# The scrap output of a sum of squares: from the row tile's lo half to the scrap tile of the weights

## Chip, core and metric

One core of a Trainium2 chip runs the whole kernel in one launch. The metric is the device time of the launch in microseconds, the median of several runs. The engines are PE (TensorE, matmuls), DVE (VectorE), ACT (ScalarE), POOL (GpSimd) and SP (SyncE, which here issues the DMAs).

## What is computed

Attention, then a mixture of experts (MoE) that is summed over all experts, then a SoLU block; from the reference:

```python
# 4 batches, 8 heads, 576 rows, head size 64; row block i sees blocks j <= i of 64
scores = scale * np.matmul(q, k.transpose(0, 1, 3, 2))
scores = np.where(mask, scores, -1000000000.0)
attn = np.exp(scores - max); attn = attn / (sum + 1e-09)
x = np.matmul(attn, v)                      # as 2304 rows x 512
p = domain_probs / (domain_probs.sum(-1, keepdims=True) + 1e-09)
for e in range(4):
    out += p[:, e:e + 1] * (np.maximum(x @ w1[e], 0.0) @ w2[e])   # 512 -> 1024 -> 512
# SoLU: h = x @ w_in; ln = layernorm(h * softmax(h)) * g_ln; return ln @ w_out
```

## The kernel before

Rows come in 18 tiles of 128 (`TILES`). Numbers that need more than 16 bits are kept as two F16 tiles, hi and lo, and a product is three matmuls (hi hi, hi lo, lo hi). Before such a split the data are multiplied by a power of two that follows from their sum of squares. That sum is what `squares` makes: ScalarE's Square, whose elementwise output is scrap and whose `accum_out` is the sum. `scale_bits` turns the sum into the power of two on VectorE (L136, L140, L143). `squares` is called from three places around the change: for the weights (`w_steps`, L212: four squares of 128x1024 for each matrix, and then L217, L219 and L221 add the four sums on VectorE and over the partitions with a matmul into the tile `tp`), for the values of attention (L859), and for the rows that attention delivers (`finish`, L1070). The first two write their scrap to `junk`, one tile of 128x1024 BF16 in a pool of one buffer. Rows of x2 later go through `split_rows` (L470), which has its scrap in a row tile too.

Attention goes by steps of two heads (four heads for the first two tiles). A step has scores (`sps`, L920 to L925), their maximum (L935 or L938) and its scaled negative `nm` (L939), exponentials into `sps` or `p32` (L979), the halves `hl` (hi L992 on ScalarE, lo L993 on VectorE), a transposing DMA `hl` to `pT`, and the products with the values (`pv`, L1021). When a tile's four steps are done, `finish` makes its MoE input in three parts: `rows` divides (`xf`, L1063), `scale` takes the squares, and `split` writes the halves into `xh` (hi L1074 on ScalarE, lo L1075 on VectorE) and sends `xh` by a transposing DMA to `xT`. `xh` comes from the pool `fp` of one buffer, so all 18 tiles share one place.

The MoE phases follow expert by expert: `hps` (L375) is the first product, `hch` (L385, L386) its halves, `ops` (L397) the second product, `acc` (L417 or L422) the sum. The weights are loaded into `stage` in four parts, and their halves are made by L231 (GpSimd) or L235 (ScalarE) with L238 (VectorE). GpSimd also splits keys, queries and values (L798, L800, L881). While attention lasts, a planner (`at1.step`, costs `tpe` and `tdv`) decides how attention's steps, the MoE units and the weights' steps follow each other in the program; it is a function of costs written into the kernel and does not look at the scrap tile. Behind it the framework's scheduler, which plays the program through a timeline of its own, chooses the order of instructions on each engine, from the dependences between tiles and the priorities. The squares' scrap is a tile like any other to it: an instruction that writes a tile waits for all who still read or write what was in that place. DMAs of SyncE stay in one order per queue that the scheduler fixes too.

Of the kernel before, what the change touches and what calls it, by code (L numbers as in the profile page):

```python
# [10 lines left out]
BF16 = mybir.dt.bfloat16  # L11
# [52 lines left out]
def tile_kernel(  # L64
# [63 lines left out]
    def squares(x, out, junk=None):  # L128

        if junk is None:  # L130
            junk = jp.tile([128, 1024], BF16, tag="junk", name="junk")[:, :x.shape[1]]
        return act.activation(out=junk, in_=x, func=AF.Square, accum_out=out)

    def scale_bits(T, bits, s, inv):

        vec.tensor_scalar(  # L136
            out=inv.bitcast(I32), in0=T.bitcast(I32), scalar1=24, scalar2=23,
            op0=ALU.logical_shift_right, op1=ALU.logical_shift_left,
        )
        vec.tensor_scalar(  # L140
            out=inv, in0=inv, scalar1=2.0 ** (64 - bits), scalar2=2.0 ** -75, op0=ALU.mult, op1=ALU.max
        )
        vec.reciprocal(out=s, in_=inv)  # L143
# [197 lines left out]
    def xtile(d, t, name):  # L341
        g, c = group(t)
        if g not in d:
            n = GROUPS[g[0]][g[1]][1]
            d[g] = xps[g[0]].tile([128, 2 * KD, 128 * n], F16, tag=f"xT{g[1]}", name=name)
        return d[g][:, :, c:c + 128]
# [397 lines left out]
    class Attention:  # L744
# [300 lines left out]
        def finish(self, t):  # L1045

            b, i = TILES[t]
            inv = sp.tile([128, 1], F32, tag="xi", name="xi")
            xf = self.fp.tile([128, NH, HD], F32, tag="xf", name="xf")
            x = xf.rearrange("p h d -> p (h d)")  # L1050
            xh = self.fp.tile([128, 2, 512], F16, tag="xh", name="xh")
            s = sp.tile([128, 1], F32, tag="xs", name="xs")

            def rows():
                ps, sums = self.xps.pop(t), self.sums.pop(t)
                rs = sp.tile([128, NH, 1], F32, tag="rs", name="rs")
                vec.tensor_scalar(
                    out=rs[:, :, 0], in0=sums, scalar1=1e-9 * 2.0 ** PBITS, scalar2=self.vSc[("z", b) if i == 0 else b],
                    op0=ALU.add, op1=ALU.mult,
                )  # L1060
                ri = sp.tile([128, NH, 1], F32, tag="ri", name="ri")
                vec.reciprocal(out=ri, in_=rs)
                vec.tensor_tensor(  # L1063
                    out=xf, in0=ps.rearrange("p (h d) -> p h d", h=NH), in1=ri.to_broadcast([128, NH, HD]),
                    op=ALU.mult,
                )

            def scale():
                T = sp.tile([128, 1], F32, tag="xt", name="xt")
                squares(x, T, xh[:, 1].bitcast(BF16))  # L1070
                scale_bits(T, 4, s, inv)

            def split():
                act.activation(out=xh[:, 0], in_=x, func=AF.Copy, scale=s)  # L1074
                vec.scalar_tensor_tensor(  # L1075
                    out=xh[:, 1], in0=x, scalar=s, in1=xh[:, 0], op0=ALU.mult, op1=ALU.subtract
                )
                sync.dma_start_transpose(out=xtile(xT, t, "xT"), in_=xh.rearrange("p a f -> p (a f)"))
                vec.tensor_scalar_mul(pt[:, t, :], pn[:, t, :], inv)

            return [rows, scale, split]


# [536 lines left out]
```

## Time and profile before

| | |
|---|---|
| runs | 1089.95, 1090.99, 1091.23 us, median 1090.99 |
| profiled execution | 1090.29 us, its span 1088.5 us |
| mean granted TensorE clock | 0.997 |
| busy: PE, DVE, ACT, POOL | 1041.5, 776.3, 511.1, 208.1 us |
| read from HBM, written | 79.47 MB, 12.06 MB |

The span is the time from the first to the last instruction in the trace; the profiled execution's own time is 1.8 us longer. Busy time is a sum over the whole span; where an engine waits has to be looked up by stretches. A share of 96% for TensorE leaves some 47 us in which it does nothing.

### The profile page before, as it was taken

How to read it: one execution, taken by the hardware profiler on the slowest of the kernel's cores; microseconds unless marked ns; L12 is line 12 of the kernel's file. 1: busy time of each engine (PE TensorE's matmuls, PEld its weight loads, DVE VectorE, ACT ScalarE, POOL GpSimd, SP SyncE). 2: the span in 40 equal slices, each digit the busy share in tenths (PEclk: the TensorE clock that was granted, in tenths of full speed). 3: DMA queues.
4: the chain of work that ended last, by engine and by line, in shares of the span. 5: the costliest groups of instructions: out<-in, count | busy, mean ns of one | idle time of the engine just before them, and what ended most of it. 6: DMA issues, size and time to landing. Idle time of an engine off the chain costs nothing.

```text
span 1088.5 us, 20680 instructions
## 1 busy us (share of the span) xinstructions
PE 1041.5 (96%) x8088; PEld 657.0 (60%) x8088; DVE 776.3 (71%) x1758; ACT 511.1 (47%) x1108; POOL 208.1 (19%) x280
## 2 busy tenths in 40 slices
PE   4679899999999999999899999999999999999998
PEld 4556666656655655655476777776766674444444
DVE  6879677748767765545786557665879558999883
ACT  5757578546755454532353334231446353323322
POOL 4967733534237311000000000000000000000000
PEclk9989999999999999999999999999999999999999
DMA  9978997566677865235331211330346312435233
GB/s 295 277 175 167 241 201 189 143 173 172 158 178 174 186 112 129 56 90 157 122 97 51 77 47 55 117 136 30 98 145 167 77 24 36 88 88 106 60 87 87
DMA packets 225745, 137.96 MB, mean 127 GB/s; under 512 B 184560, under 2 KB 193008, under 8 KB 225648
## 3 DMA queue, kind: packets, MB, share of 16 engines
q1 hardware_dynamic: 225648, 136.65, 50.3%
q8 instruction: 63, 1.03, 0.4%
q14 instruction: 34, 0.28, 0.1%
HBM read 79.47 MB, written 12.06 MB: 84 GB/s over the span
## 4 chain that ended last, share of the span: by engine, by line
PE 84%; DMA 6%; DVE 4%; POOL 3%; ACT 1%; issue 1%; SPq 0%; DVEq 0%; ACTq 0%; POOLq 0%
PE ops L397 31%; PE hps L629 14%; PE hps L375 14%; PE o L1536 9%; PE h L1470 9%; PE pv L1021 3%; DMA pT<-hl 3%; PE sps L920 2%; PE sps L923 2%; DMA xT<-xh 1%; POOL ks L800 1%; DMA raw<-in_w_dram 1%; DMA x2T<-xh 1%; DMA near<-in_kT_dram 1%; DMA vraw<-in_vC_dram 1%
## 5 line engine op out<-in xcount | busy, mean ns | idle before, releaser
L397 PE MATMUL ops<-wt,hch 128*128 128x512 f16 x1728 | 393.1, 379 | 2.4 <-DVE wt L238 1.4
L397 PEld LDWEIGHTS <-hch 128*128 128x128 f16 x1728 | 166.1, 98 | 187.4 <-issue 6.7
L375 PE MATMUL hps<-xT,wt 128*128 128x384 f16 (+1 forms) x1536 | 216.1, 290 | 6.3 <-DVE hch L386 3.9
L375 PEld LDWEIGHTS <-wt 128*128 128x128 f16 x1536 | 126.5, 100 | 64.4 <-issue 6.1
L979 ACT ACTIVATE p<-sps,nm 128x320 f32<-128x320 f32 (+3 forms) x120 | 70.1, 587 | 85.1 <-DVE nm L939 75.4
L993 DVE TENSOR_TENSOR hl<-p,hl 128x320 f16<-128x320 f32 (+3 forms) x120 | 75.6, 650 | 37.3 <-ACT hl L992 37.2
L629 PEld LDWEIGHTS <-S 128*128 128x128 f16 x1152 | 96.0, 98 | 3.0 <-issue 0.9
L1536 PE MATMUL o<-wt,lt 128*128 128x512 f16 (+1 forms) x456 | 95.6, 368 | 0.0
L1470 PE MATMUL h<-wt,x2T 128*128 128x512 f16 x432 | 95.5, 379 | 0.0
L238 DVE SCALAR_TENSOR_TENSOR wt<-stage,ws,wt 128x1024 f16<-128x1024 f32 (+1 forms) x64 | 82.9, 1304 | 7.4 <-ACT wt L235 4.3
L422 DVE SCALAR_TENSOR_TENSOR acc<-ops,coef,acc 128x512 f32<-128x512 f32 x54 | 40.4, 748 | 66.4 <-PE ops L397 66.3
L920 PE MATMUL sps<-ks,qhi 128*128 128x288 f32 (+3 forms) x160 | 69.1, 433 | 10.7 <-DVE hl L993 7.5
L629 PE MATMUL hps<-T,S 128*128 128x192 f16 x864 | 76.3, 246 | 0.0
L629 PEld LDWEIGHTS <-wt 128*128 128x128 f16 x864 | 72.8, 98 | 5.8
L642 ACT ACTIVATE stu<-hps 128x384 f32<-128x384 f32 x72 | 34.6, 482 | 86.5 <-PE hps L629 86.3
L1536 PEld LDWEIGHTS <-lt 128*128 128x128 f16 x456 | 44.6, 98 | 48.9
L1470 PEld LDWEIGHTS <-x2T 128*128 128x128 f16 x432 | 42.3, 98 | 51.0
L386 DVE SCALAR_TENSOR_TENSOR hch<-hps,hch 128x384 f16<-128x384 f32 (+1 forms) x98 | 52.8, 540 | 21.9 <-ACT hch L385 21.8
L647 ACT ACTIVATE hch<-stc 128x384 f16<-128x384 f32 x72 | 37.4, 521 | 63.5 <-DVE stc L655 63.2
L385 ACT ACTIVATE hch<-hps 128x384 f16<-128x384 f32 (+1 forms) x98 | 46.9, 481 | 39.5 <-PE hps L375 39.4
L1021 PE MATMUL pv<-v,pT 128*128 128x64 f16 x1392 | 56.6, 196 | 8.9 <-DMA pT<-hl 8.8
L1021 PEld LDWEIGHTS <-pT 128*128 128x128 f16 x1392 | 51.6, 100 | 20.5 <-DMA pT<-hl 10.8
(163 smaller groups left out, 1534.6 us busy)
## 6 DMA issues: line engine op xcount, KB each, us to landing
stage<-in_w_dram SPq DMA_DIRECT2D x50, 512.0 KB, 5.9
raw<-in_qT_dram SPq DMA_DIRECT2D x34, 256.0 KB, 3.1
vraw<-in_vC_dram SPq DMA_DIRECT2D x30, 256.0 KB, 3.2
raw<-in_kT_dram SPq DMA_DIRECT2D x24, 288.0 KB, 3.5
raw<-in_w_dram SPq DMA_DIRECT2D x24, 256.0 KB, 4.1
raw<-in_w_in_dram SPq DMA_DIRECT2D x8, 512.0 KB, 4.7
raw<-in_w_out_dram SPq DMA_DIRECT2D x8, 512.0 KB, 4.2
stage<-wf SPq DMA_DIRECT2D x8, 512.0 KB, 6.6
```

The lines of the kernel that those rows point to most:

```text
L238: stage["last"] = vec.scalar_tensor_tensor(out=lo, in0=r, scalar=stage[key, "s"], in1=hi, op0=ALU.mult, op1=ALU.subtract)
L375: pe.matmul(ps[:, j * n:j * n + n], w[:, a, kk, f * 128:(f + 1) * 128], x[:, b * KD + kk, c0:c0 + n], start=(m == 0), stop=(m == 3 * KD - 1),)
L385: marks["A"] = nc.scalar.activation(out=h[:, 0, :n], in_=ps[:, :n], func=AF.Relu)
L386: marks["D"] = nc.vector.scalar_tensor_tensor(out=h[:, 1, :n], in0=ps[:, :n], scalar=0.0, in1=h[:, 0, :n], op0=ALU.max, op1=ALU.subtract)
L397: pe.matmul(ps, hch[f][:, a, o0:o0 + 128], w[:, b, f, :], start=(m == 0), stop=(m == 3 * KF - 1))
L629: i = pe.matmul(ps[x][:, jj * HT:jj * HT + HT], lhs(a, kk, jj), rhs(b, kk), start=start, stop=(m == 5), skip_group_check=not first or jj > 0,)
L920: pe.matmul(o, q, rhs, start=True, stop=False)
L979: act.activation(out=src if direct else dst, in_=src, func=AF.Exp, bias=nm[:, j + x:j + x + 1], scale=SCALE, accum_out=sums[:, h:h + 1],)
L993: anc["D"] = vec.tensor_tensor(out=lo, in0=pf, in1=hi, op=ALU.subtract)
L1021: pe.matmul(o, tt[:, a * nch + c, :], v[:, bb, hs], start=(m == 0), stop=(m == total - 1))
L1470: pe.matmul(ps[:, half], x[:, a * KD + kk, c:c + 128], w[:, b, kk, half * 512:half * 512 + 512], start=(m == 0), stop=(m == 3 * KD - 1),)
L1536: pe.matmul(ps, tt[:, x * KF + f], w[:, y, f, c], start=(m == 0), stop=(m == 3 * KF - 1))
```

## The change

One line in `finish`: the squares of a tile's 128x512 rows no longer name a place for their scrap, so `squares` takes the first 512 columns of `junk`. Number, engine, size and type of the 18 squares are as before.

```diff
             def scale():
                 T = sp.tile([128, 1], F32, tag="xt", name="xt")
-                squares(x, T, xh[:, 1].bitcast(BF16))
+                squares(x, T)
                 scale_bits(T, 4, s, inv)
```

So the square no longer writes `xh`: it need not wait until the DMA of the previous tile has read `xh`, and the lo half (L1075) need not wait for it as a writer of the same bytes. It writes `junk` instead, behind the square that wrote `junk` before it, on the same engine. With these dependences the scheduler's order differs on every engine, from about 35 to 230 us by the clock of before: on PE in rows 132 to 3136 of 15778, on DVE up to row 335 of 1760, on ACT up to 229 of 850, on POOL from 35 up to 132 of 285, on SP up to 129 of 391. Behind that the engines' rows are the same. Tiles are numbered in order of their making, and each `finish` now makes one more, so that names differ by a few: `sps_1228` of before is `sps_1232`, `hl_1269` is `hl_1273`, `tp_1390` is `tp_1394`, `stage_1116` is `stage_1119`, `pT_1501` is `pT_1505`.

ScalarE, before, at 43 us in the trace: the squares of the first weight matrix of expert 1 (`stage_1116`), two of the four shown, among the steps of the third and fourth tile.

```order
L979 ACTIVATE sps_602,sums_509<-sps_602,nm_603 128x192
L132 ACTIVATE junk_1232,wt4_1117<-stage_1116 128x1024
L132 ACTIVATE junk_1317,wt4_1117<-stage_1116 128x1024
L979 ACTIVATE sps_651,sums_509<-sps_651,nm_652 128x192
L132 ACTIVATE xh_533,xt_540<-xf_532 128x512
L992 ACTIVATE hl_618<-sps_602 128x192
L992 ACTIVATE hl_703<-sps_651 128x192
```

ScalarE in the change, at the place where `finish` of a later tile has its square (`junk_1211` from `xf_1202`): here stand the four squares of that matrix (`stage_1119`), with the exponentials of `sps_1232` between.

```order
L132 ACTIVATE junk_1211,xt_1210<-xf_1202 128x512
L417 ACTIVATE acc_1311<-ops_1286,c0_1284 128x512
L132 ACTIVATE junk_1236,wt4_1120<-stage_1119 128x1024
L132 ACTIVATE junk_1321,wt4_1120<-stage_1119 128x1024
L979 ACTIVATE p32_1274,sums_1084<-sps_1232,nm_1233 128x448
L979 ACTIVATE p32_1278,sums_1084<-sps_1232,nm_1233 128x448
L1074 ACTIVATE xh_1203<-xf_1202,xs_1204 128x512
L132 ACTIVATE junk_1323,wt4_1120<-stage_1119 128x1024
L992 ACTIVATE hl_1273<-p32_1274 128x448
L992 ACTIVATE hl_1273<-p32_1278 128x448
L132 ACTIVATE junk_1325,wt4_1120<-stage_1119 128x1024
L979 ACTIVATE p32_1336,sums_1084<-sps_1319,nm_1320 128x448
```

The four squares moved some fifty rows back on ScalarE, from rows 44, 45, 56 and 58 to rows 93, 94, 98 and 101.

VectorE, before: the sum over the four squares' results (L217, `wt1_1388`), at 57.81 us in the trace.

```order
L386 SCALAR_TENSOR_TENSOR hch_656<-hps_655,hch_656 128x384
L238 SCALAR_TENSOR_TENSOR wt_560<-stage_268,ws_270,wt_560 128x1024
L386 SCALAR_TENSOR_TENSOR hch_656<-hps_724,hch_656 128x384
L217 TENSOR_REDUCE wt1_1388<-wt4_1117 128x1
L935 TENSOR_REDUCE sps_777<-sps_777 128x2
L386 SCALAR_TENSOR_TENSOR hch_780<-hps_779,hch_780 128x256
```

VectorE in the change, the same instruction (`wt1_1392`), behind the maximum of `sps_1390` and the lo halves of `hl_1273`.

```order
L1075 SCALAR_TENSOR_TENSOR xh_1203<-xf_1202,xs_1204,xh_1203 128x512
L938 TENSOR_REDUCE nm_1391<-sps_1390 128x1
L939 TENSOR_SCALAR nm_1391<-nm_1391 128x1
L993 TENSOR_TENSOR hl_1273<-p32_1274,hl_1273 128x448
L993 TENSOR_TENSOR hl_1273<-p32_1278,hl_1273 128x448
L217 TENSOR_REDUCE wt1_1392<-wt4_1120 128x1
L221 COPY wt2_1396<-tp_1394 128x1
```

PE, before: the matmul that reads it, into `tp_1390`, between the scores `sps_1315` and the first product `hps_1450` of expert 1.

```order
L920 MATMUL sps_1315<-ks_440,qhi_1021 128x448
L923 MATMUL sps_1315<-ks_440,qlo_1022 128x448
L925 LDWEIGHTS mr_88
L925 MATMUL sps_1315<-mc_89,mr_88 128x64
L920 MATMUL sps_1315<-ks_443,qhi_1021 128x448
L923 MATMUL sps_1315<-ks_443,qlo_1022 128x448
L925 LDWEIGHTS mr_88
L925 MATMUL sps_1315<-mc_89,mr_88 128x64
L219 MATMUL tp_1390<-wt1_1388,ones_87 128x1
L375 LDWEIGHTS wt_415
L375 MATMUL hps_1450<-xT_477,wt_415 128x128
```

PE in the change: the same matmul, into `tp_1394`, behind the products of `pT_1181` and the scores `sps_1390`.

```order
L1021 LDWEIGHTS pT_1181
L1021 MATMUL pv_1346<-v_459,pT_1181 128x64
L920 MATMUL sps_1390<-ks_396,qhi_1221 128x288
L923 MATMUL sps_1390<-ks_396,qlo_1222 128x288
L925 LDWEIGHTS mr_88
L925 MATMUL sps_1390<-mc_89,mr_88 128x64
L920 MATMUL sps_1390<-ks_396,qhi_1221 128x288
L923 MATMUL sps_1390<-ks_396,qlo_1222 128x288
L219 MATMUL tp_1394<-wt1_1392,ones_87 128x1
L375 LDWEIGHTS wt_415
L375 MATMUL hps_1454<-xT_478,wt_415 128x128
```

It moved behind 48 products with `pT_1094` and `pT_1181` and behind `sps_1390`, and stands ahead of `hps_1454` as before. A little earlier on PE the 24 matmuls of `ops_1282` stand before as 8 behind `sps_1114`, 14 behind `sps_1228` and 2 behind the products of `pT_1001`; in the change as 11 ahead of `sps_1117` (`sps_1114` of before), 11 behind it, and 2 behind `sps_1232`.

SyncE, before: the transposes of attention's halves (`pT`) and the loads of the second weight matrix of expert 1 (`stage_2501`, four parts of 512 KB), at 100 to 123 us in the trace.

```order
L94 DMA_TRANSPOSE pT_1340<-hl_1331 128x14x128
L94 DMA vraw_1636<-in_vC_dram 128x512
L94 DMA_TRANSPOSE pT_1501<-hl_1406 128x18x128
L94 DMA raw_1790<-in_qT_dram 128x512
L94 DMA stage_2501<-in_w2_dram 128x2x512 x2
L94 DMA raw_1658<-in_kT_dram 128x576
L94 DMA stage_2501<-in_w2_dram 128x2x512 x2
L94 DMA raw_1738<-in_kT_dram 128x576
L94 DMA_TRANSPOSE pT_1651<-hl_1584 128x18x128
L94 DMA_TRANSPOSE xT_1214<-xh_1615 128x8x128
```

SyncE in the change (`stage_2508`; `pT_1505` is `pT_1501` of before):

```order
L94 DMA_TRANSPOSE pT_1282<-hl_1273 128x14x128
L94 DMA_TRANSPOSE pT_1344<-hl_1335 128x14x128
L94 DMA raw_1536<-in_kT_dram 128x576
L94 DMA vraw_1641<-in_vC_dram 128x512
L94 DMA stage_2508<-in_w2_dram 128x2x512 x3
L94 DMA_TRANSPOSE pT_1505<-hl_1410 128x18x128
L94 DMA_TRANSPOSE xT_1218<-xh_1619 128x8x128
L94 DMA_TRANSPOSE pT_1656<-hl_1588 128x18x128
L94 DMA raw_1663<-in_kT_dram 128x576
L94 DMA raw_1743<-in_kT_dram 128x576
```

Three of the four parts moved ahead of that transpose, the fourth behind three more transposes; `vraw` and `raw` loads moved among them.

## Rows read from the trace of the kernel before

**Rows 1.** The page: engines' busy time, and what the chain that ended last consists of.
```profile
PE 1041.5 (96%) x8088; PEld 657.0 (60%) x8088; DVE 776.3 (71%) x1758; ACT 511.1 (47%) x1108; POOL 208.1 (19%) x280
...
PE 84%; DMA 6%; DVE 4%; POOL 3%; ACT 1%; issue 1%; SPq 0%; DVEq 0%; ACTq 0%; POOLq 0%
```

**Rows 2.** Stretches: start:end and length, busy us (x instructions) by engine, PEclk, DMA share, GB/s.
```profile
53.00:71.00 18.00, 11.93 (x113) 7.65 (x109) 14.74 (x27) 9.85 (x29) 17.38 (x16) 1.00 0.61 122
71.00:77.00 6.00, 5.23 (x47) 4.59 (x47) 3.78 (x8) 4.01 (x12) 2.73 (x4) 0.50 1.05 276
77.00:103.00 26.00, 26.00 (x347) 19.84 (x345) 22.20 (x49) 21.26 (x51) 14.69 (x19) 0.98 0.84 182
103.00:106.00 3.00, 0.72 (x18) 0.46 (x17) 3.00 (x4) 1.95 (x4) 2.91 (x4) 1.00 0.76 130
106.00:123.00 17.00, 17.00 (x204) 13.07 (x199) 15.92 (x35) 9.96 (x22) 13.88 (x20) 1.00 1.00 251
123.00:135.00 12.00, 8.23 (x150) 6.75 (x148) 4.39 (x12) 5.40 (x20) 9.21 (x17) 1.00 1.15 218
151.00:1088.50 937.50, 929.34 (x6823) 567.09 (x6820) 657.94 (x1487) 415.47 (x846) 101.89 (x146) 1.00 0.44 110
```

**Rows 3.** TensorE's waits, 98 to 152 us: total us, times, longest.
```profile
PE pv L1021 <- DMA pT<-hl: 5.9, 4, 2.3
PE hps L375 <- DMA xT<-xh: 1.9, 1, 1.9
```

**Rows 4.** Chain that ended last, 76 to 150 us: start, us, what.
```profile
82.29 1.73 PE ops L397 x8
...
89.16 0.43 PE ops L397 x2
...
90.57 0.20 PE tp L219 x2
...
92.00 1.42 PE pv L1021 x48
...
114.91 19.15 DMA pT<-hl x3
```

**Rows 5.** The row tile xh: duration min/median/max in ns; idle time before, by releaser.
```profile
L132 ACT ACTIVATE xh<-xf x18: 614/629/646, 31.3 to 490.3; 128x512 bf16<-128x512 f32 x18
...
  DMA xT<-xh: 5.5, 1
```

**Rows 6.** The scrap tile junk, 20 to 110 us, same columns.
```profile
L132 ACT ACTIVATE junk<-vr x5: 620/629/660, 27.2 to 33.0; 128x512 bf16<-128x512 f32 x5
```

**Rows 7.** ScalarE in order of time: start, us, line, tiles, count, idle before.
```profile
43.27 1.06 ACT L132 ACTIVATE junk<-stage 128x1024 bf16<-128x1024 f32 x1
...
87.99 0.63 ACT L979 ACTIVATE p<-sps,nm 128x448 f32<-128x448 f32 x1 [1.16 <-DVE nm L939]
...
89.22 1.04 ACT L992 ACTIVATE hl<-p 128x448 f16<-128x448 f32 x2
90.16 0.68 ACT L417 ACTIVATE acc<-ops,c 128x512 f32<-128x512 f32 x1
...
150.23 0.63 ACT L132 ACTIVATE xh<-xf 128x512 bf16<-128x512 f32 x1 [5.47 <-DMA xT<-xh]
```

**Rows 8.** VectorE in order of time, same columns.
```profile
85.65 1.10 DVE L935 TENSOR_REDUCE sps<-sps 128x2 f32<-128x896 f32 x1 [0.51 <-PE sps L925]
86.66 1.15 DVE L993 TENSOR_TENSOR hl<-p,hl 128x448 f16<-128x448 f32 x2
...
92.23 0.75 DVE L938 TENSOR_REDUCE nm<-sps 128x1 f32<-128x576 f32 x1
```

**Rows 9.** DMA issues, 20 to 140 us: count, median us from issue to landing.
```profile
pT<-hl SPq DMA_TRANSPOSE x23, 4.4
```

**Rows 10.** DMA issues, 110 to 123 us, same columns.
```profile
pT<-hl SPq DMA_TRANSPOSE x1, 9.1
```

**Rows 11.** SyncE's DMA issues in order of time.
```profile
110.31 0.90 SPq L94 DMA_DIRECT2D stage<-in_w_dram  x2
```

## Prediction

> **What bounds the kernel now.** I read the page first. TensorE is busy 96% of the span and holds 84% of the chain that ended last [rows 1], so a change is worth what it adds to or takes from TensorE's waits. The table by stretches says where those are [rows 2]. From 151 us on, 929.34 of 937.50 us are busy: nothing to gain there, and a delay that gets that far reaches the end. The waits that can move lie ahead: 18.00 - 11.93 = 6.07 us in 53 to 71, 3.00 - 0.72 = 2.28 in 103 to 106, 12.00 - 8.23 = 3.77 in 123 to 135 [rows 2], and 1.9 for a row tile's transpose, which ends at 150.2 [rows 3, 7]. Between 77 and 103 TensorE has no wait at all, nor between 106 and 123.
>
> The three stretches have three limits. In 53 to 71 GpSimd is busy 17.38 of 18 us. In 77 to 103 TensorE itself is the limit. In 106 to 135 it is the DMA engines, busy share 1.00 and 1.15 [rows 2], and the chain there is one piece of 19.15 us through three transposing loads [rows 4].
>
> **The edit itself.** The square costs the same in either place: 629 ns into the row tile, 629 ns into junk [rows 5, 6]. What goes is the square's wait until the transposing DMA has read the previous row tile. The trace has that wait once, 5.5 us [rows 5], before the square at 150.23 [rows 7]. At that moment TensorE's own wait of 1.9 us for that same DMA's data ends [rows 3], and that transfer doesn't start sooner because a later tile's square does. The next write of the row tile, L1074, needs the DMA to be done anyway. So the direct gain is 0; its upper bound is the 1.9 us of that wait.
>
> **What moves.** Without that dependence the scheduler lays out 35 to 230 us anew; behind that the engines' rows are the same. The sum is that of the new order, walked with the durations of before.
>
> *36 to 76 us.* ScalarE loses four squares of 128x1024 here (they go to 90 us and later), and VectorE's and GpSimd's work changes places. GpSimd has the same work in 17.38 busy of 18 us, so what it delivers last can't come much earlier. Some tiles come 2 to 3 us sooner, the first quarter of the second weight matrix later. Bounds: a gain of all 6.07 us; a loss of 3.3, if three of GpSimd's operations (17.38 / 16 = 1.09 each) now stand ahead of one that TensorE waits for. I take **-1.0**, near nothing, since the amount of GpSimd's work is the limit and stays.
>
> *77 to 98 us.* Here new waits arise. (a) Eleven matmuls of L397 now stand ahead of sps_1117 (sps_1114 of before). One takes 1.73 / 8 = 0.216 us, so these scores, which ended at 82.29 [rows 4], end 2.4 us later, at 84.7 on the clock of before. Behind them stand one maximum (1.10), two exponentials (0.63 each), the halves (0.5) and a subtraction (0.6) [rows 7, 8]: the hi and lo rows are whole at 88.8 if nothing else lies between, at 90.2 if it takes the 5.5 us that it took before (82.29 to 86.66 + 1.15). The transposing load takes 4.4 us [rows 9], so its data are there from 93.2 to 94.6. TensorE gets to them at about 91.1: its work ahead of them is that of before (48 pv matmuls from 92.00 in 1.42, half of them ahead) less the 1.6 us of tp, hps and sps from 90.4 on that now come later [rows 4]. Wait: 2.1 to 3.5; I take 2.7. (b) Then come five matmuls of sps_1390 and the tp matmul. Before, tp ran at 90.57 without a wait [rows 4], since VectorE had formed its operand long ahead. Now that operand stands behind the maximum of sps_1390 (0.75) and two subtractions (1.15) [rows 8], 1.9 us at least; and it needs the last of the four squares. ScalarE starts their row when the last of 24 matmuls of L397 is done: before these ended at 89.16 + 0.43 [rows 4] and acc started 0.57 later; now they end at 89.8, so acc starts at 90.4. Then acc 0.6, two squares at 1.16, two exponentials 0.55 to 0.63, the copy of the rows 0.7, a square, the halves 1.04, a square with its readout 1.25 [rows 7]: 8.0 us, 98.4. TensorE is there at 93.8 + 0.7 (the other 24 pv) + 0.9 (sps_1390: the 1.6 above without tp and hps) = 95.4. Wait: 2.0 to 4; I take 3.0. Behind tp stand all of hps_1454 and the scores after it, so nothing fills it. Together **+5.7**.
>
> *98 to 106 us.* The 2.28 us for a transposing load at 105.5 shrink, since what feeds it moved less than TensorE did; two short waits of 0.8 and 0.65 stay by the walk. **-0.8** (0 to -2.28). TensorE is then 3.9 us late at 106.
>
> *106 to 135 us.* DMA decides. Before, pT_1501 is issued ahead of the four 512 KB loads that start at 110.31 [rows 11]; now three of the four are ahead of it. From 110.31 to the landing of the last transpose of the chain, 114.91 + 19.15 = 134.06 [rows 4], there are 23.75 us at a full share. The change puts one more transpose into them, and takes out one 256 KB load (1.0 us at the 251 GB/s of this stretch). A transpose takes 4.4 in the median [rows 9]; if half of it lies beside the next one, the landing is 4.4 / 2 - 1.0 = 1.2 later, if none does 3.4. I take 2.3. TensorE comes 3.9 late and waits there for data that are only 2.3 late, so 1.6 of the 5.9 - 2.28 = 3.6 us waited there for pT [rows 2, 3] are given back: **-1.6**. Behind 135 the delay is carried to the end.
>
> Sum: -1.0 + 5.7 - 0.8 - 1.6 = **+2.3 us**. The profiled execution took 1090.29 (span 1088.5) and would take 1092.6; the median of the runs is 0.70 above it, so I expect **1093.3**.
>
> **The rivals.** What a measurement of this kernel can tell from no change is about 0.2%, 2.2 us.
>
> *Given back whole.* If the transpose moved into the full DMA stretch costs nothing there, the landing comes no later, and all of the 3.6 us is given back: +0.3, 1091.3 (1090 to 1092). For it: the total of the transfers hardly changes. Against: the share of 1.00 and 1.15, and the transpose that stood behind the four loads took 9.1 us where 4.4 is the median [rows 9, 10].
>
> *Not given back, or a lower clock.* After the waits of 53 to 71 the granted clock was 0.50 (the 1.2 GHz level) in 71 to 77: 5.23 us of busy time there [rows 2] would be 2.6 at 2.4 GHz. After two waits of 2.7 and 3.0 us close together it could fall again: 2.6 more, and pT_1505 late by 9.1 - 4.4 = 4.7 times three of four loads, 3.5, instead of any give-back. +3.9 + 2.6 is 1097.5; 1095 to 1098. Against: in 103 to 106 TensorE waited 2.28 of 3 us, and the clock stayed at 1.00.
> The Trainium skill (TensorE: Matmul & The Clock Gate, "What's actually happening") has the throttled rate as the default that activity releases, so after idle time the array may run at half rate; the row of 71 to 77 agrees, that of 103 to 106 shows that not every wait does it.
>
> *Faster.* The stretch of 36 to 76 gains more than I allow: with the squares gone from ScalarE and the row tile's lo half sooner, half of the 6.07 us goes (3.0), and the clock doesn't fall in 71 to 77 (2.6). That is -5.6 in place of -1.0, and -2.3 in all: 1088.7. It decides from 3.3 us of gain in that stretch on. For it: the waits of 53 to 71 are the largest that there are, and the order changes on all engines there. Against: GpSimd's 17.38 of 18.
>
> That the edit does nothing at all (the same order) is excluded by the rows of the order.
>
> **Chances.** Forecast, +1 to +4: 0.47 (own range 1092 to 1095; above 0.2% with 0.32, within it 0.15). Given back whole: 0.18 (same 0.15, faster 0.03). Not given back: 0.16, slower. Faster: 0.19 (faster 0.17, same 0.02). So slower 0.48, same 0.32, faster 0.20. The range is 1089.0 to 1097.5: below it lies about half of the faster case (0.10), above it a third of the third one (0.05), so that 0.15 is left out.
>
> **What would show it.** In the trace of the change: no square waits for xT<-xh, and nothing is gained by it at 150; four junk<-stage squares between 90 and 99 where ScalarE is without a pause; a TensorE wait for a pT of about 2.7 us ahead of sps_1390, and one of about 3 us ahead of tp that ends with VectorE's L217; fewer than 3.6 us waited for pT between 123 and 135; from 151 on the same busy share. I am wrong if TensorE is still without a wait between 77 and 98 (then the walk by durations is wrong, and ScalarE's or the load's lag was shorter), if it waits under 3 us between 53 and 71 (the faster case), or if a stretch behind 151 has changed.

## The result, and the profile after

The change makes the kernel slower: 1097.42 us in the median (1095.95 to 1099.37, four runs) beside 1090.47 of the kernel before on the same chip, a ratio of 1.0073 [1.0053, 1.0094], some 8 us (7.0 between the two medians). I had forecast 1093.3 us, +2.3. The time lies in the range (1089.0 to 1097.5) at its upper end, where the rival "not given back, or a lower clock" stands. The profiled execution took 1099.37 us, 2 above the median.

The stretches of the change, with the columns of [rows 2]:

```profile
53.00:71.00 18.00, 13.56 (x149) 9.32 (x147) 14.11 (x25) 6.86 (x22) 17.28 (x16) 1.00 0.71 159
71.00:77.00 6.00, 3.89 (x35) 2.67 (x32) 2.38 (x6) 4.02 (x12) 2.47 (x5) 0.78 0.86 212
77.00:103.00 26.00, 20.72 (x223) 16.17 (x221) 17.35 (x44) 20.35 (x50) 7.43 (x12) 0.76 0.66 144
103.00:106.00 3.00, 2.86 (x34) 2.54 (x32) 2.67 (x3) 3.00 (x5) 1.46 (x3) 0.66 1.24 263
106.00:123.00 17.00, 14.45 (x180) 11.14 (x176) 15.69 (x31) 11.56 (x24) 15.12 (x18) 1.00 0.69 172
123.00:135.00 12.00, 9.61 (x179) 8.89 (x180) 6.60 (x15) 4.81 (x13) 6.40 (x11) 1.00 1.02 217
151.00:1097.60 946.60, 938.39 (x6904) 572.53 (x6901) 666.90 (x1503) 420.36 (x860) 107.50 (x154) 1.00 0.45 111
```

Read the first number after the length (TensorE's busy time) with the granted clock, third from the end. 77 to 103 was 26.00 busy at 0.98; it is now 20.72 at 0.76, so both waits and a low clock are there. 106 to 123 had no wait and has one of 2.55 us. From 151 on 8.2 us are idle, as before (8.2): whatever is lost is lost ahead of that.

TensorE in order of time, the two new waits in brackets:

```profile
94.66 1.36 PE L1021 MATMUL pv<-v,pT 128*128 128x64 f16 x24 [2.49 <-DMA pT<-hl]
...
96.94 0.44 PE L923 MATMUL sps<-ks,qlo 128*128 128x288 f32 x1
100.17 0.59 PE L219 MATMUL tp<-wt,ones 128*128 128x1 f32 x2 [2.79 <-DVE wt L217]
100.62 2.62 PE L375 MATMUL hps<-xT,wt 128*128 128x128 f16 x23
...
123.72 1.05 PE L1021 MATMUL pv<-v,pT 128*128 128x64 f16 x30 [3.27 <-DMA pT<-hl]
```

ScalarE, the row of squares:

```profile
91.29 1.04 ACT L132 ACTIVATE junk<-stage 128x1024 bf16<-128x1024 f32 x1
...
97.31 1.05 ACT L132 ACTIVATE junk<-stage 128x1024 bf16<-128x1024 f32 x1
98.26 0.20 ACT L132 ACTIVATION_READ_ACCUMULATOR junk<-stage 128x1 f32 x1
```

VectorE, what forms the operand of tp:

```profile
97.42 0.76 DVE L938 TENSOR_REDUCE nm<-sps 128x1 f32<-128x576 f32 x1 [1.19 <-PE sps L923]
98.21 0.15 DVE L939 TENSOR_SCALAR nm<-nm 128x1 f32<-128x1 f32 x1
98.29 1.76 DVE L993 TENSOR_TENSOR hl<-p,hl 128x448 f16<-128x448 f32 x2
99.97 0.14 DVE L217 TENSOR_REDUCE wt<-wt 128x1 f32<-128x4 f32 x1
```

SyncE's queue, at the place of the fourth term:

```profile
113.14 1.41 SPq L94 DMA_DIRECT2D stage<-in_w_dram  x3
114.66 6.97 SPq L94 DMA_TRANSPOSE pT<-hl  x1
```

The two waits are the forecast ones, of nearly the forecast size: 2.49 for the transpose (2.7), 2.79 for tp (3.0). The last of the squares ends at 98.46 with its readout, where the walk had 98.4. It is not what ended the wait for tp, though: L217 runs at 99.97, behind the maximum of `sps_1390`, which had waited for TensorE's scores until 97.42, and behind two subtractions of together 1.76 us. And the matmuls between the two waits take longer: a 128x288 product of the scores (L920) takes 0.59 us at 95.83 and 0.38 at 106.49. In each stretch of low clock the granted clock is 0.50, the 1.2 GHz level. Last, pT_1505 behind three loads makes TensorE wait 3.27 us at 123.72.

### The profile page after: what moved, and what is told of

It reads as the page before. It is cut to its first block, busy times and chain, and to the rows that moved or that the text cites. A ratio compares the mean times of both kernels' runs of the same rounds, so it can differ in the third digit from the quotient of the medians.

```text
span 1097.6 us, 20675 instructions
## 1 busy us (share of the span) xinstructions
PE 1044.3 (95%) x8088; PEld 659.3 (60%) x8088; DVE 779.5 (71%) x1758; ACT 512.5 (47%) x1108; POOL 207.6 (19%) x280
## 4 chain that ended last, share of the span: by engine, by line
PE 80%; DMA 6%; DVE 5%; POOL 4%; issue 2%; ACT 1%; SPq 1%; DVEq 0%; POOLq 0%; ACTq 0%
PE ops L397 31%; PE hps L629 14%; PE hps L375 11%; PE o L1536 9%; PE h L1470 8%; DMA pT<-hl 3%; PE pv L1021 3%; PE sps L920 2%; PE sps L923 1%; POOL ks L800 1%; DVE hch L386 1%; POOL ks L798 1%; DMA x2T<-xh 1%; POOL v L881 1%; SPq L94 1%
## 5 line engine op out<-in xcount | busy, mean ns | idle before, releaser
L397 PE MATMUL ops<-wt,hch 128*128 128x512 f16 x1728 | 393.2, 379 | 3.2 <-DVE wt L238 1.7
L397 PEld LDWEIGHTS <-hch 128*128 128x128 f16 x1728 | 166.4, 98 | 188.0 <-issue 7.1
L375 PE MATMUL hps<-xT,wt 128*128 128x384 f16 (+1 forms) x1536 | 219.8, 292 | 2.7 <-DVE hch L386 1.8
L993 DVE TENSOR_TENSOR hl<-p,hl 128x320 f16<-128x320 f32 (+3 forms) x120 | 75.8, 650 | 38.6 <-ACT hl L992 38.2
L920 PE MATMUL sps<-ks,qhi 128*128 128x288 f32 (+3 forms) x160 | 69.8, 437 | 12.3 <-DVE hl L993 7.7
```

The costliest lines, as they stand in the source:

```text
L375: pe.matmul(ps[:, j * n:j * n + n], w[:, a, kk, f * 128:(f + 1) * 128], x[:, b * KD + kk, c0:c0 + n], start=(m == 0), stop=(m == 3 * KD - 1),)
L397: pe.matmul(ps, hch[f][:, a, o0:o0 + 128], w[:, b, f, :], start=(m == 0), stop=(m == 3 * KF - 1))
L920: pe.matmul(o, q, rhs, start=True, stop=False)
L993: anc["D"] = vec.tensor_tensor(out=lo, in0=pf, in1=hi, op=ALU.subtract)
```

## What the order shows, and the theories

Why do four squares of a weight move fifty rows back because a row square changed its scrap? `junk` has one buffer, and the numbers in its names tell the order in which the program makes the tiles: `junk_1211`, tile 3's row square, comes ahead of `junk_1236`, the first square of the weights. Writers of one buffer keep the program's order. Before, the row square wrote elsewhere, and the scheduler let the weights' squares run ahead of it to ScalarE's row 44. In the change they have to wait for tile 3's rows, on row 91.

*Theory A*: this chain of squares, and the order that the scheduler makes from it, costs the time; where the square writes costs nothing. *Rival B*: the freed row tile does it, as the square and the lo half start at other times and the order changes by that. Later runs ask which part of the new order costs: the late squares, the matmuls of L397 ahead of the scores, or the three loads ahead of pT_1505, each by its wait or by the clock.

## The experiments

Times are given as ratios to the kernel before on the same chip with their 95% interval; 0.001 is 1.1 us. In some kernels each engine is bound to a list of its instructions, so that the scheduler lays nothing out anew:

```diff
+    for e, order in pins().items():
+        m = made[e]
...
+        for a, b in zip(order, order[1:]):
+            if b < a or True:
+                after(m[b], m[a])
```

Where a list is edited, the diff shows the move, with the names that stand in it cut short. "Own scrap" is the edit of the first run.

### An own scrap for the rows

```diff
-            junk = jp.tile([128, 1024], BF16, tag="junk", name="junk")[:, :x.shape[1]]
+            junk = jp.tile([128, 1024], mybir.dt.float8e4, tag="junk", name="junk")[:, :x.shape[1]]
...
-                squares(x, T, xh[:, 1].bitcast(BF16))
+                squares(x, T, jp.tile([128, 512], BF16, tag="rows", name="rscrap"))
```

The weights' scrap has 8 bits here, to make room.

> The 18 squares of finish write a scrap tile of their own (the weights' scrap becomes 8-bit to make room for it), so they wait neither for the row tile's DMA nor for the weights' squares. Theory A (one place for all scrap makes the scheduler keep the squares of both kinds in program order, so that the weights' squares of expert 1 stand behind the square of tile 3): they stand early again, no tp wait between 90 and 101, time 1088 to 1093. Rival B (what costs is that the square no longer holds to the row tile, so that everything is laid out anew): 1095 to 1098, as the change.

Measured: 1.0045 [1.0030, 1.0060]. The median, 1096.35 us, lies where rival B had it, and there is no wait for tp, as theory A had it. What came is a third order, which waits 2.28 us for a pT at 150.63 and has the low clock from 151 to 159. So without the chain of squares a new order comes about as well, and it costs some 5 us.

### The chain without the scrap

```diff
-        return act.activation(out=junk, in_=x, func=AF.Square, accum_out=out)
+        prev, marks["sq"] = marks.get("sq"), act.activation(out=junk, in_=x, func=AF.Square, accum_out=out)
+        return after(marks["sq"], prev) or marks["sq"] if prev is not None else marks["sq"]
```

> The kernel before, scrap in the row tile as before, but each square is bound to follow the square before it in the program (an order on ScalarE alone, no wait is added). Theory A: the expert-1 squares stand behind tile 3's, tp waits 2 to 3 us near 97 to 100, time 1094 to 1099. Rival B: the row tile is held as before, so 1089 to 1092.

Measured: 1.0057 [1.0038, 1.0077], with the waits of the change (2.67 for pT, 2.65 for tp), as theory A had it. The scrap stays in the row tile here, so binding the order of the squares alone is enough for the scheduler to make an order with a loss like the change's.

### Which tiles

All but tile 3; tile 3 alone; the first four; the last 14:

```diff
-                squares(x, T, xh[:, 1].bitcast(BF16))
+                squares(x, T, None if t != 3 else xh[:, 1].bitcast(BF16))
...
+                squares(x, T, None if t == 3 else xh[:, 1].bitcast(BF16))
...
+                squares(x, T, None if t < 4 else xh[:, 1].bitcast(BF16))
...
+                squares(x, T, xh[:, 1].bitcast(BF16) if t < 4 else None)
```

> The change in 17 of the 18 tiles; only the square of tile 3 writes to its row tile as before. By the order the four weights' squares then stand behind tile 2's square, some 25 rows of ScalarE earlier than in the change. Theory A: tp's operand is ready in time, no tp wait and no lower clock at 95 to 105, time 1089 to 1094. Rival B: 1095 to 1098, since 17 of 18 row tiles are freed.

> The change in one tile of 18: only the square of tile 3 writes to the weights' scrap. Theory A: the order of the four weights' squares is that of the change, tp waits 2 to 3 us, time 1094 to 1099. Rival B: 1089 to 1092, since 17 of 18 squares are as before.

> The edit in the first four finish tiles only (tiles 0 to 3 write the squares of their rows to the weights' scrap; the 14 later tiles as before). Nothing is bound; the order on every engine comes out as that of the change. If the shared scrap of the first four tiles is the whole cause, the ratio is the change's: 1.006 to 1.009 (1097 to 1100.5). If the 14 later tiles add to it or give some back, it lies outside: below 1.005 or above 1.010.

> The edit in the last 14 of 18 tiles, the first four as before; nothing is bound, and the scheduler's order comes out the same as before on every engine. If only the order costs: 1.000, within 0.2%. If the square's freedom from the row tile's DMA is worth something (the one wait of 5.5 us at 150 is among these 14 tiles): up to 1.9 us faster.

Measured, in this order: 1.0072 [1.0047, 1.0098], 1.0069 [1.0048, 1.0090], 1.0069 [1.0047, 1.0091], 1.0002 [0.9985, 1.0018]. The last 14 tiles keep the order of before on every engine and cost nothing. The first four have the change's order on every engine, name by name but for the numbers, and its time: they carry the whole of it. Theory A missed twice here. Without tile 3 there is no tp wait, as it had it, but a fourth order with a pT wait of 4.70 us at 151.84, and the loss did not go. With tile 3 alone the time is the forecast one, but not its cause: the four squares are as late as in the change (the last ends at 98.8), and still TensorE does not wait for tp. It waits for GpSimd's `qlo` (2.67 us at 95.13) and for transposes (2.60 at 99.27, 3.16 at 129.03).

### The order of before, with the squares freed

Own scrap, and every engine bound to the order of before.

> As e1_own (the rows' squares have a scrap tile of their own, nothing waits for the row tile's DMA), but every engine and the DMA queue are bound to the order of the kernel before. Theory C (the order alone is what costs; where the scrap lies costs nothing): 1089 to 1092. Rival D (the scrap's place, or the freed squares, cost by themselves): 1094 to 1097, as e1_own.

Measured: 0.9990 [0.9971, 1.0008]. The scrap's place and the freed row tile are worth nothing; only the order costs. What is left of rival B is that freeing the row tile makes the scheduler lay out a new order. The run with the last 14 tiles shows the same for the scrap in `junk`, and that the one wait for the row tile's DMA at 150 was worth nothing.

### Pieces of the change taken back

Bound to the order of the change. First one transpose ahead of the three loads; then own scrap with the squares and L217 where they were before; the same and the lo halves of `hl_1273` ahead of the maximum; the same and TensorE's scores as before.

```diff
 SP
+pT_1505<-hl_1410
 stage_2508<-in_w2_dram x3
-pT_1505<-hl_1410
 ACT
+junk<-stage_1119 x4
 junk_1211<-xf_1202
-junk<-stage_1119 x4
 DVE
+hl_1273<-p32 x2
 nm_1391<-sps_1390
-hl_1273<-p32 x2
 PE
+sps_1117<-ks,qhi
 ops_1286<-wt,hch x11
-sps_1117<-ks,qhi
```

> The change, bound to its own order on every engine, with one DMA moved: pT_1505 is issued ahead of the three 512 KB loads of stage_2508 and not behind them. If these loads cost what the trace shows (TensorE waits 3.27 us for that transpose at 123.7), that wait goes and the time is 1093 to 1095. If the wait only moves to the next transposes of a stretch that DMA limits, 1096 to 1099.

> The change's order on every engine, with own scrap for the rows' squares, and only the four squares of expert 1's first matrix and the sum behind them (L217) put back to where they stand before, near 43 to 58 us. If the late operand of tp and the clock that falls with it cost what the trace shows (2.8 us of wait, some 2 to 4 us of low clock at 95 to 105): 1090 to 1094. If the delay is only moved to the next DMA that TensorE waits for: 1095 to 1098.

> As x2_early_squares (the change's order, own scrap, squares and L217 early), and on VectorE the two lo halves of hl_1273 stand ahead of the maximum of sps_1390, as before. Theory E (the loss is in attention's chain of scores, halves, transposes and products, which the new order makes late: pT_1282 is issued at 101.16 where it was at 91.05): pT_1282 is issued 3 to 5 us earlier, the wait of 3.0 us at 104.1 goes, time 1091 to 1094. If the chain was already late by the matmuls of ops_1286 ahead of the scores: 1095 to 1098.

> As y1_lo_first, and on TensorE the 24 matmuls of ops_1286 stand behind the scores again as before (8 behind sps_1117, 14 behind sps_1232, 2 behind the products of pT_1004). Theory E: with the scores 2.4 and 4.8 us earlier the chain is where it was: 1089 to 1092. If the order behind 106 us costs by itself: 1094 to 1097.

Measured: 1.0050 [1.0033, 1.0067], 1.0067 [1.0042, 1.0092], 1.0075 [1.0050, 1.0100], 1.0112 [1.0092, 1.0132]. No single piece gives the loss back, and the third and fourth, at medians of 1098.41 and 1103.15 us, are slower than either case that was expected for them (the third by 0.4 us only). In the second the wait for tp is gone, and a wait for the next transpose stands in its place:

```profile
104.12 0.95 PE L1021 MATMUL pv<-v,pT 128*128 128x64 f16 x24 [3.04 <-DMA pT<-hl]
```

In the first the wait for pT_1505 is gone (its products run at 117.45). The transpose after it (`pT_1656`) is issued at 117.95, with only `xT_1218` between it and the three loads, and its wait is 4.79 us where the change has 1.68 at 129.38:

```profile
117.45 1.04 PE L1021 MATMUL pv<-v,pT 128*128 128x64 f16 x30
126.31 1.78 PE L1021 MATMUL pv<-v,pT 128*128 128x64 f16 x30 [4.79 <-DMA pT<-hl]
```

So this wait moved to the next transpose too.

### Pieces of the change put into the order of before

Own scrap, bound to the order of before, with one move each: the matmuls of L397 ahead of the scores (72 matmuls of TensorE stand as in the change); the three loads ahead of pT_1501; both; the four squares, L217 with what hangs on it, and on TensorE tp with the nine matmuls of hps_1450 that follow, at the change's places; all three.

```diff
 PE
-sps_1114<-ks,qhi
 ops_1282<-wt,hch x11
+sps_1114<-ks,qhi
 SP
-pT_1501<-hl_1406
 stage_2501<-in_w2_dram x3
+pT_1501<-hl_1406
 ACT
-junk<-stage_1116 x4
 acc_1307<-ops_1282
+junk<-stage_1116 x2
 xh_1200<-xf
+junk<-stage_1116 x2
 DVE
-wt1_1388<-wt4_1117
 nm_1387<-nm_1387
+wt1_1388<-wt4_1117
 PE
-tp_1390<-wt1_1388
 pv<-v,pT_1178 x24
+tp_1390<-wt1_1388
```

> The order of before on every engine (own scrap for the rows' squares, which cost nothing so), and on TensorE alone the 72 matmuls around sps_1114 and sps_1228 stand as in the change: 11 of ops_1282 ahead of sps_1114, 11 behind it, sps_1228 behind the products of pT_954 and pT_1001. Theory E: attention's chain is late by 2 to 5 us, time 1092 to 1096. If the change's loss is in other moves: 1089 to 1091.

> The order of before on every engine (own scrap), and on the DMA queue alone three of the four 512 KB loads of stage_2501 are issued ahead of pT_1501. By the trace of the change (a wait of 3.27 us for that transpose): TensorE waits 2 to 4 us more between 110 and 124, time 1091 to 1094. If the transpose is not needed so soon there: 1089 to 1091.

> The order of before (own scrap) with both single moves: 11 matmuls of ops_1282 ahead of sps_1114 and the rest as in the change, and three loads of stage_2501 ahead of pT_1501. Each alone cost 1.0027, 2.9 us. If delays add: 1.0054, some 1096. If the second is hidden behind the first (TensorE comes later to the transpose, so the loads are no longer in its way): 1.0027 to 1.0035, 1093 to 1094.

> The order of before (own scrap) with the four squares of expert 1's first matrix moved behind acc_1307 and behind the split of xh_1200 on ScalarE, the sum of them (L217) and what follows from tp behind the maximum of sps_1386 on VectorE, and the tp matmul with the nine matmuls of hps_1450 behind the products of pT_1178 on TensorE, as in the change. If the term of the sum holds (3.0 us of wait for tp) and nothing gives it back: 1093 to 1095. If attention's chain sets the time and tp only waits beside it: 1090 to 1092.

> All three moves in the order of before (own scrap). If these three are what the change costs: 1097 to 1099, ratio 1.006 to 1.008. If other moves of the new order are needed for it: 1093 to 1096.

Measured: 1.0027 [1.0011, 1.0043], 1.0027 [1.0011, 1.0044], 1.0047 [1.0030, 1.0063], 1.0071 [1.0052, 1.0090], 1.0120 [1.0101, 1.0139]. So 2.9, 2.9, 5.1, 7.7 and 13.1 us: in this order the prices add up (5.1 + 7.7 = 12.8). The late squares alone cost as much as the whole change, and the three together 5 us more; if prices add there too, the rest of the change's order gives some 5 us back, which no run shows by itself. The last two took more than either case that was expected for them. The loads by themselves give a longer wait for their transpose, on TensorE:

```profile
116.92 1.78 PE L1021 MATMUL pv<-v,pT 128*128 128x64 f16 x30 [4.91 <-DMA pT<-hl]
```

But TensorE's waits from 106 to 151 are 5.1 us in all there, where the kernel before has 5.7: this wait took the place of later ones. What that stretch has more in this profile is the low clock behind the wait, 2.9 us (0.50 from 116 to 122), where the three profiles of before's order lose 0 to 1.0.

The late squares by themselves, TensorE and VectorE:

```profile
98.39 0.59 PE L219 MATMUL tp<-wt,ones 128*128 128x1 f32 x2 [6.39 <-DVE wt L217]
98.84 3.90 PE L375 MATMUL hps<-xT,wt 128*128 128x128 f16 x35
```

```profile
98.17 0.16 DVE L217 TENSOR_REDUCE wt<-wt 128x1 f32<-128x4 f32 x1 [3.35 <-ACT junk L132]
```

Here the last square does end VectorE's wait, and TensorE's with it. With no pT wait ahead of it the wait for tp is 6.39 us, as long as the two of the change together and a little more, and twice the 3.0 of the forecast. Its stretches:

```profile
92.00:98.00 6.00, 0.00 (x1) 0.00 (x0) 1.62 (x7) 5.62 (x14) 2.66 (x5) 0.67 0.99 171
98.00:104.00 6.00, 5.61 (x46) 5.47 (x47) 2.60 (x12) 2.48 (x6) 0.05 (x1) 0.50 0.22 42
```

### The wait filled with idle matmuls

Matmuls whose result nobody reads, in an unused part of `pv`: in the change's order 36 ahead of the pT wait and 60 ahead of tp; in the run with the late squares 100 ahead of tp.

```diff
+                fill.extend(nc.tensor.matmul(ps[:, 256:384], mc, mc, start=True, stop=True) for z in range(NBF if (t, p) == (4, 1) else 0))
```

> The change, bound to its own order, with work that does nothing put into TensorE's two waits ahead of pT_1181 (36 matmuls of 128 columns) and ahead of tp (60): they write a part of the pv tile that is written again later. The waits stay. If the lower clock in 95 to 105 is what the trace says (busy time at 0.50), TensorE keeps the 2.4 GHz level there and the time is 1092 to 1095; if the low clock is hidden by the DMAs behind it, 1096 to 1099.

> The order before with the late squares alone (as in the run that put just the four squares, L217 with its chain on DVE and the tp transposes late: +7.7 us), and 100 matmuls of 128 columns whose result nobody reads ahead of the tp transposes, on an unused part of the pv tile. The idle 6.4 us ahead of tp becomes mostly busy, so the granted clock should stay at 1.00 there. If the low clock of 94 to 104 carries a share of the 7.7 us, the time falls to +3 to +5 (1093 to 1096 at a kernel before of 1090.5). If the wait itself carries it (the clock lost only time in which PE would have waited anyway), it stays at +6.5 to +9 (1097 to 1099.5).

Measured: 1.0068 [1.0045, 1.0091] and 1.0052 [1.0034, 1.0071]. In the second the clock is up until 130 us, and the 35 matmuls of hps behind tp take 2.12 us where they took 3.90:

```profile
91.07 5.75 PE L1041 MATMUL pv<-mc 128*128 128x128 bf16 x100
97.62 0.38 PE L219 MATMUL tp<-wt,ones 128*128 128x1 f32 x2 [0.81 <-DVE wt L217]
97.86 2.12 PE L375 MATMUL hps<-xT,wt 128*128 128x128 f16 x35
```

It is 5.7 us slower than before in place of 7.7. The intervals overlap, so a share of 2 us for the low clock behind tp is what the medians say and is not settled. In the first the clock stays up from 73 to 103; then TensorE waits 3.35 us for a transpose, after which the clock is low all the same, from 103 to 110, at a cost of 3.0 us. There the low clock only moved, and the time stayed that of the change.

## Why the prediction was wrong

One profile of each order could mislead, since the clock falls in other places from run to run. There are three profiles of before's order (before, own scrap bound to it, the last 14 tiles) and two of the change's (the change, the first four tiles). Stretches of the kernel before:

```profile
0.00:77.00 77.00, 46.07 (x394) 39.29 (x394) 59.64 (x143) 48.83 (x142) 56.68 (x65) 0.96 0.91 248
77.00:106.00 29.00, 26.72 (x363) 20.31 (x362) 25.20 (x52) 23.22 (x54) 17.60 (x22) 0.99 0.83 176
106.00:151.00 45.00, 39.35 (x521) 30.30 (x517) 33.53 (x78) 23.58 (x68) 31.90 (x48) 1.00 1.06 236
```

of the change:

```profile
0.00:77.00 77.00, 44.31 (x397) 37.26 (x398) 58.96 (x140) 43.99 (x132) 56.74 (x65) 0.98 0.91 249
77.00:106.00 29.00, 23.58 (x253) 18.70 (x252) 20.02 (x46) 23.35 (x54) 8.89 (x15) 0.75 0.72 157
106.00:151.00 45.00, 38.04 (x548) 30.80 (x545) 33.63 (x72) 24.82 (x65) 34.50 (x48) 1.00 0.87 200
```

and of the first four tiles:

```profile
0.00:77.00 77.00, 44.44 (x409) 37.36 (x409) 59.75 (x141) 44.38 (x133) 56.55 (x65) 1.00 0.89 248
77.00:106.00 29.00, 23.13 (x289) 17.90 (x289) 22.62 (x48) 25.57 (x58) 12.25 (x17) 0.88 0.80 167
106.00:151.00 45.00, 39.01 (x529) 30.57 (x526) 34.23 (x77) 23.88 (x65) 34.38 (x49) 1.00 0.92 217
```

Length less busy time is what TensorE waits; busy time by (1 - clock), summed over steps of 1 us of the same view, is what it loses to the low clock. The first border is put at 85 us for this, since a stretch of low clock lies across 77 in the kernel before (71 to 78) and in the change (74 to 81); from 77 to 85 TensorE waits for 0.02 us at most in all five. Worked out so, in us, waits + clock:

```
             before  bound   last14 | change  first4 | means: difference  predicted
0 to 85      30.9+3.0 30.5+1.7 31.2+1.7 | 32.7+3.2 32.6+0.0 |  +1.2   -1.0
85 to 106     2.3+0.0  2.6+0.0  2.4+0.0 |  5.4+3.7  5.9+2.4 |  +6.2   +4.9
106 to 151    5.7+0.0  5.5+1.0  5.9+1.0 |  7.0+0.0  6.0+0.0 |  +0.1   -1.6
151 to 200    0.1+0.0  0.0+0.8  0.0+0.7 |  0.9+0.0  0.8+0.0 |  +0.3    0
```

The sum, before rounding, is +7.9, beside spans that differ by 8.4 in the mean ((1097.6 + 1095.5) / 2 against 1088.2). Of it 6.6 are waits and 1.3 are clock: behind the two new waits the clock costs 3.0 more, and elsewhere the change's order loses 1.7 less to it than before's. With 6.8 and 2.4 us of clock in two profiles of one order, that share is rough.

The step that failed is this: the sum let the new order give time back at two places, -1.0 ahead of 76 us and -1.6 behind 106, and put the low clock behind the two new waits at nothing. The runs show +1.2 and +0.1 at the two places, and +3.0 for that clock; the waits between 85 and 106 came out 1.7 below the sum and took part of it back.

- *The edit itself, 0*: right. The own scrap in before's order (0.9990) and the last 14 tiles (1.0002) show it.
- *77 to 106, +5.7 - 0.8*: the waits came where and about as long as forecast, and the 2.28 us at 105.5 went almost whole and not by 0.8 (0.14 left in 103 to 106), which makes +3.2 of waits in place of +4.9. The clock was left out of the sum: it is 0.50 from 95 to 105 in the change and from 95 to 101 in the first four tiles, which costs 3.7 and 2.4 us, +3.0 in the mean. The prediction had 2.6 for this in a rival, with "against" from the one wait of 103 to 106 that kept the clock: the size was right and stood on the wrong side. The rival gave two waits close together as the reason; that is not shown, since in the change the clock is at 0.50 from 95 on, behind the first of the two.
- *The wait for tp, 3.0 in that sum*: its size is partly luck. The walk had TensorE there at 95.4 and the last square at 98.4 as what it waits for. TensorE came at 97.4, and the wait ended with VectorE's row, which the walk had at "1.9 us at least"; the square had been done for 1.5 us.
- *106 to 135, -1.6 given back*: wrong, +0.1. pT_1505 waits behind three loads, 9.0 us from its issue at 114.66, as the one behind four loads had 9.1 [rows 10], and TensorE, which came late, waits 3.27 us again. The rival had 3.5; the loads alone cost 2.9.
- *36 to 76, -1.0*: +1.2. The waits grew by some 1.8 us (one for VectorE's L993 at 41.66 is 4.32 where 2.19 stood before), and a lower clock loss than in the profiles of before's order took 0.6 back. I had not looked at 36 to 53 at all. And the 6.07 us of 53 to 71 belong to that one profile: the two others with before's order have 4.40 and 4.13 there, and the change has 4.44.
- *Chances*: the forecast's case had 0.47, the one that came 0.16. The two terms that were to give time back and the one put at nothing erred to the same side.

Shown: that the order costs and not the place of the scrap; that the first four tiles carry it; that the late squares alone are enough for 7.7 us in before's order. Not shown: that they are what costs in the change's own order, since put back there they give nothing clear of the noise (1.0067). Open: why no single piece taken back helps within the change's order. What the runs show is only that another transpose's wait takes the place (3.04, 4.79 us), and that four other orders of this stretch lose 5 to 8 us as well. None of the 18 kernels was faster than the one before; the nearest, bound to its order, is equal to it.

## What to carry to other kernels

A scrap tile of one buffer is a lock: all who write it keep the program's order, so give a stream that must run ahead (here the weights' squares) a scrap that no later stream shares, and look at whom the sharing makes wait, not at what the write costs. Here that was not enough by itself: the own scrap cost 1.0045 as long as the scheduler was free, and nothing with the old order. When an edit of no direct worth lets a scheduler lay out a tuned stretch anew, price the order: bind the new kernel to the old order, and the difference is the order's. And put the low clock behind a new wait into the sum, with its spread (here 2.4 and 3.7 us for one order), not beside it; and let no term give time back without a row that shows where.

## What I had not expected of the hardware

- The same instructions in the same order lose 6.8 us to the low clock in one profile and 2.4 in another (first 240 us), with the stretches of 0.50 in other places: 75 to 81 and 94 to 105 in the change, 95 to 101 in the first four tiles. Before's order lost 3.0, 3.4 and 3.4.
- 100 small matmuls in a wait of 6.4 us keep the clock at 1.00 there and behind it until 130, and two stretches of low clock turn up later in that run, 0.58 in 130 to 134 and 0.57 in 140 to 144; the run without them has 1.00 in the first and 0.57 in 138 to 142.
